# Decode attention: loading K and V two heads per transfer, their rows interleaved

## The chip, the cores and the metric

One core of one Trainium2 chip. The metric is device microseconds of one execution, each version run several times. A kernel's "ratio" below is the mean time of its runs over the mean of the other kernel's runs of the same rounds, so it is not quite the ratio of the medians that are quoted beside it.

## The reference, cut to what matters

Two layers, each an attention block and a small MLP, run on one token. Every attention block reads the last 4,096 rows of the K and of the V cache of all 32 heads, 192 bf16 each:

```python
W = min(4096, max(256, Sk // 4))                 # 4096
k = k_cache[:, :, Sk - W:, :]; v = v_cache[:, :, Sk - W:, :]
scores = einsum("bhqd,bhkd->bhqk", q, k) * Dh ** -0.5
o = einsum("bhqk,bhkd->bhqd", softmax(scores), v)
# ... then  @ wo, and the MLP: layernorm, w3, gelu, w4.  Both layers share K, V and all weights.
```

One head's K or V is 4,096 × 192 × 2 B = 1.5 MB. The kernel reads 216 MB in all, and there is one query: nearly everything is a load.

## The kernel before

The arena is 11 "cells" of 12,288 B per partition. One head's K or V fills a cell: partition p holds 32 consecutive cache rows, so a transfer is 128 packets of 12,288 contiguous bytes, 8 for each of the 16 DMA engines.

```python
def load_k(layer, h):
    t = take(("k", layer, h))                    # the cell that was freed first
    nc.sync.dma_start(t[:], A_k_cache[0, h, s0:Sk, :].rearrange("(p j) d -> p (j d)", p=P))
    return t
```

VectorE transposes K in 32×32 blocks of 4-byte words (two bf16 together), so that a score matmul reads every second bf16 of a row, in four quarters of a head:

```python
nc.vector.transpose(Tu, Ku[:, :, q * NY:(q + 1) * NY])
# ... scores():
nc.tensor.matmul(ST_ps[r:r + QW, :]..., lhsT=Q[:, n, :], rhs=T4[:, :, f, :, t], ...)
```

The product with V has two columns of probabilities at a time, and one transpose of the result for each head:

```python
nc.tensor.matmul(O_ps[r:r + 2, :], lhsT=PT[:, hq, 2 * i:2 * i + 2],
                 rhs=v_pair(V, h, 2 * i * Dh, 2 * Dh), start=(i < 4), stop=(i >= NB - 4))
# ... after the 16 matmuls of a head:
nc.vector.transpose(o_sb[:], O_ps.rearrange("p (e a c) -> p e c a", e=2, c=NA))
```

Layer 0 keeps the transposed K of heads 0 to 6 and parts of V in on-chip memory for layer 1, so cells are scarce around the layer change. The loads are one stream in a fixed order, all issued by SP; each waits only for its cell to be free. At the end of layer 1 come wo, w3 and w4.

Of the kernel before, what the change touches and what calls it, by code (L numbers as in the profile page):

```python
# [8 lines left out]
BF16 = mybir.dt.bfloat16  # L9
# [26 lines left out]
def kernel(  # L36
# [38 lines left out]
    NKX = 6  # L75
    NKEEP, NCELL = 7, 11
# [13 lines left out]
    cells = ctx.enter_context(tc.tile_pool(name="cells", bufs=1))  # L90
# [15 lines left out]
    kx = const.tile([P, VN], BF16, name="kx")  # L106

# [3 lines left out]
    free = deque(range(NCELL))  # L111
    cell_of = {}

    def take(key):
        i = free.popleft()
        cell_of[key] = i
        return cells.tile([P, FREE], BF16, tag=f"cell{i}", name=f"cell{i}")

    def give(key):
        free.append(cell_of.pop(key))  # L120
# [7 lines left out]
    def load_k(layer, h):  # L128
        t = take(("k", layer, h))
        nc.sync.dma_start(t[:], A_k_cache[0, h, s0:Sk, :].rearrange("(p j) d -> p (j d)", p=P))  # L130
        return t

    def load_v(layer, h):
        t = take(("v", layer, h))
        src = A_v_cache[0, h, s0:Sk, :].rearrange("(p j) d -> p (j d)", p=P)
        cut = (2 * VW,) if h == VP else (FREE - VN,) if h == VX else ()
        if layer == 1 and h in GROUPS[layer][-1][-2:]:
            cut = FREE // 2,
        i = 0
        for e in cut + (FREE,):  # L140
            kept_v = h == VP or h == VX and i > 0
            if layer == 0 or not kept_v:
                nc.sync.dma_start(v_pair(t, h, i, e - i), src[:, i:e])
            i = e
        return t
# [23 lines left out]
    def load_w3(layer):  # L169

        t = take(("w3", layer))
# [9 lines left out]
    def load_w4(layer):  # L181

        t = take(("w4", layer))
# [19 lines left out]
    def layer_stream(layer):  # L203
# [3 lines left out]
        def k_item(hh):  # L207
            if layer == 0 or hh >= NKEEP:
                seq.append(("k", layer, hh))

        def v_item(hh):
            if (layer, hh) == (1, VC):
                return
# [48 lines left out]
    ones = const.tile([P, P], F32, name="ones")  # L262
    nc.vector.memset(ones[:], 1.0)
    Lf = wx_sb[:, 0:2 * P].bitcast(F32).rearrange("p (j i) -> p j i", j=4)
    nc.gpsimd.memset(Lf, 0.0)
    for base in (0, -1, -64, -65):
# [10 lines left out]
    even = const.tile([P, 1], F32, name="even")  # L277
    nc.vector.reduce_sum(even[:], ident[:].rearrange("p (m two) -> p m two", two=2)[:, :, 0], axis=AX.X)
    lo = const.tile([P, 1], F32, name="lo")
    nc.vector.reduce_sum(lo[:], ident[:, 0:64], axis=AX.X)  # L280
    maskq = const.tile([P, 4], F32, name="maskq")
    nc.vector.tensor_tensor(out=maskq[:, 0:1], in0=lo[:], in1=even[:], op=ALU.mult)
    nc.vector.tensor_tensor(out=maskq[:, 1:2], in0=lo[:], in1=maskq[:, 0:1], op=ALU.subtract)
    nc.vector.tensor_tensor(out=maskq[:, 2:3], in0=even[:], in1=maskq[:, 0:1], op=ALU.subtract)
    nc.vector.tensor_scalar(out=maskq[:, 3:4], in0=lo[:], scalar1=-1.0, scalar2=1.0, op0=ALU.mult, op1=ALU.add)
    nc.vector.tensor_tensor(out=maskq[:, 3:4], in0=maskq[:, 3:4], in1=maskq[:, 2:3], op=ALU.subtract)
    blkm = const.tile([P, NM], F32, name="blkm")
    nc.vector.reduce_sum(blkm[:], ident[:].rearrange("p (m b) -> p m b", m=NM), axis=AX.X)
# [3 lines left out]
    eps1 = const.tile([P, 1], F32, name="eps1")  # L292
    nc.vector.memset(eps1[:], eps)

    hm = const.tile([P, QH], F32, name="hm")
    nc.vector.tensor_reduce(out=hm[:], in_=ident[:].rearrange("p (q x m) -> p x q m", q=4, m=NM)[:, 0:QH],
                            op=ALU.add, axis=AX.XY)

    QW = QH * NM
    QHEAD = NCOL * QW  # L300
    QSLOT = QH * (QHEAD + NM)
# [10 lines left out]
    xT = const.tile([P, ND], F32, name="xT0")  # L312
    xT_ps = psm.tile([P, ND], F32, tag="psm")
    nc.tensor.transpose(xT_ps[:, :], x_rf, ident[0:ND, 0:ND])
    rs0 = const.tile([P, 1], F32, name="rs0")
    nc.vector.tensor_scalar(out=xT[:], in0=xT_ps[:], scalar1=1.0, scalar2=None, op0=ALU.mult,
# [3 lines left out]
    def ln_center(x, rowsum):  # L320

        mean_ps = psm.tile([P, 1], F32, tag="psm")
        nc.tensor.matmul(mean_ps[:], lhsT=ones[:], rhs=rowsum[:, 0:1], start=True, stop=True)
# [3 lines left out]
        xcf = big.tile([P, ND], F32, name="xcf")  # L327
        nc.vector.scalar_tensor_tensor(out=xcf[:], in0=mean_ps[:, 0:1].broadcast_to([P, ND]), scalar=-1.0 / D,
                                       in1=x[:], op0=ALU.mult, op1=ALU.add)
        junk = sm.tile([P, ND], F32, tag="ln_junk")  # L330
        ssq = sm.tile([P, 1], F32, tag="ln_ssq")
        nc.scalar.activation(junk[:], xcf[:], ACTF.Square, accum_out=ssq[:, 0:1])

        def total():
            var_ps = psm.tile([P, 1], F32, tag="psm")
            nc.tensor.matmul(var_ps[:], lhsT=ones[:], rhs=ssq[:, 0:1], start=True, stop=True)
            return var_ps
# [3 lines left out]
    def power(var, mul, bias, tag):  # L341

        ln_t = big.tile([P, 1], F32, tag=tag + "_ln")
        nc.scalar.activation(ln_t[:], var, ACTF.Ln, bias=bias, scale=mul)
        r = big.tile([P, 1], F32, tag=tag)
        nc.scalar.activation(r[:], ln_t[:], ACTF.Exp, scale=-0.5)
# [7 lines left out]

    kept = {}
    area = [None, 0]

    def transpose_quart(layer, h, q):
# [5 lines left out]
        Ku = Kn[:].bitcast(U32).rearrange("p (j y b) -> p j y b", j=NJ4, b=32)  # L364
# [4 lines left out]
        else:  # L369
            if area[0] is None:  # L370
                area[0] = take(("area", layer))
            T = area[0][:, area[1] * QUART:(area[1] + 1) * QUART]
            area[1] = (area[1] + 1) % NT
# [6 lines left out]
    def qproj_steps(c, xc, part=None, row=None):  # L380
# [49 lines left out]
        def block():  # L430
            nh = n * P // Dh
            h0 = 4 * (t0 - c * QT) // NCOL
            diag = Qblk[:, c % 2].rearrange("p (h r) -> p h r", h=QH)[:, h0:h0 + nh, 0:QHEAD]
# [6 lines left out]

    def scores(h, Ts, q0, ST_ps, hq):

        ng = NGK // NT
        Q = Qblk[:, h // QH % 2, hq * QHEAD:(hq + 1) * QHEAD].rearrange("p (f x) -> p f x", x=QW)
# [26 lines left out]
    def softmax_steps(n, ST_ps, sc):  # L471
        held = {}

        def part_max():
            pm = big.tile([P, 1], F32, name="pm")
            nc.vector.tensor_reduce(out=pm[:], in_=ST_ps, op=ALU.max, axis=AX.X)
            held["pm"] = pm

        def turn_max():
            pmT_ps = psm.tile([1, P], F32, tag="psm")  # L480
            nc.tensor.transpose(pmT_ps[0:1, :], held["pm"][:, 0:1], ident[:, :])
            held["pmT"] = pmT_ps

        def full_max():
            ngm = big.tile([1, 2 * QH], F32, name="ngm")
            nc.vector.tensor_reduce(out=ngm[:], in_=held["pmT"][0:1, :].rearrange("o (q x m) -> o x q m", q=4, m=NM),
                                    op=ALU.max, axis=AX.XY, negate=True)
            held["PrT"] = o_bytes[:, SW:2 * SW]

            wide = held["PrT"][0:1, :].bitcast(F32)  # L490
            nc.vector.tensor_scalar(  # L491
                out=wide.rearrange("o (q x m) -> o q x m", q=4, m=NM),
                in0=ngm[:].unsqueeze(1).unsqueeze(3).broadcast_to([1, 4, 2 * QH, NM]),
                scalar1=sc[0:1, 0:1], scalar2=None, op0=ALU.mult)
            held["w"] = wide

        def spread_max():
            nb_ps = psm.tile([P, 1], F32, tag="psm")
            nc.tensor.matmul(nb_ps[:], lhsT=held["w"],  # L499
                             rhs=ones[0:1, 0:1], start=True, stop=True)  # L500
            nb_sb = big.tile([P, 1], F32, name="nb_sb")
            nc.scalar.copy(nb_sb[:], nb_ps[:])  # L502
            Pr = o_bytes[:, 0:SW]
            lpart = big.tile([P, 1], F32, name="lpart")
            nc.scalar.activation(out=Pr, in_=ST_ps, func=ACTF.Exp,  # L505
                                 bias=nb_sb[:, 0:1], scale=sc[:, 0:1], accum_out=lpart[:, 0:1])
            held["Pr"], held["l"] = Pr, lpart

        def turn_p():
            nc.vector.transpose(held["PrT"], held["Pr"])  # L510
            lh = big.tile([P, QH], F32, name="lh")
            nc.vector.tensor_scalar(out=lh[:], in0=hm[:], scalar1=held["l"][:, 0:1], scalar2=None, op0=ALU.mult)
            held["lh"] = lh

        def swap():
            ng = NGK // NT
            PT_ps = psm.tile([P, n, NJ4, NGK], F32, tag="psm")
            src = held["PrT"].rearrange("p (g j i) -> p i j g", g=ng, j=NJ4)
# [4 lines left out]
            PT = big.tile([P, n, NJ4 * NGK], BF16, name="PT")  # L523
            nc.scalar.copy(PT[:].rearrange("p h c -> p (h c)"), PT_ps[:].rearrange("p h j g -> p (h j g)"))  # L524
            l_ps = psm.tile([P, QH], F32, tag="psm")
            nc.tensor.matmul(l_ps[:], lhsT=ones[:], rhs=held["lh"][:], start=True, stop=True)  # L526
            held["lps"] = l_ps
            return PT

        def recip():  # L530
            lq = big.tile([P, QH], F32, name="lq")
            rl = sm.tile([P, 1], F32, name="rl")
            nc.vector.scalar_tensor_tensor(out=lq[:], in0=held["lps"][:], scalar=1.0, in1=blkm[:],
# [24 lines left out]
    def pv(layer, h, hq, PT, mid=None):  # L558
# [3 lines left out]
        NB = NJ4 * NGK // 2  # L562
        for i in range(NB):
            if mid is not None and i == NB // 2:
                mid()
            r = 32 * (i % 4)
            nc.tensor.matmul(O_ps[r:r + 2, :], lhsT=PT[:, hq, 2 * i:2 * i + 2],  # L567
                             rhs=v_pair(V, h, 2 * i * Dh, 2 * Dh), start=(i < 4), stop=(i >= NB - 4))
# [3 lines left out]
        else:  # L572
            give(("v", layer, h))
        nc.vector.transpose(o_sb[:], O_ps.rearrange("p (e a c) -> p e c a", e=2, c=NA))  # L574

    def o_fold(h, oT, rl, add=False):
        r = slice(32 * (h % QH), 32 * (h % QH) + 32)
        oT_ps = psm.tile([P, NA], F32, tag="psm")
        if not add:
            for e in range(2):  # L580
                nc.tensor.matmul(oT_ps[r, :], lhsT=Lq[:], rhs=o_sb[:, e, :, e], start=(e == 0), stop=(e == 1))  # L581
# [3 lines left out]
        nc.vector.tensor_add(o2[:], o_sb[:, 0, :, 0], o_sb[:, 1, :, 1])  # L585
# [53 lines left out]
    def attention(layer, x_cur, rs_cur, x_new, z_new, rs_new, ss_new):  # L639
# [3 lines left out]
        junk = sm.tile([P, ND], F32, tag="ln_junk")  # L643
# [3 lines left out]
        sc = sm.tile([P, 1], F32, name="sc")  # L647

        def softmax_scale():
            rstd = power(total()[:, 0:1], 1.0 / D, eps1[:], "rstd")  # L650
            nc.vector.tensor_scalar(out=sc[:], in0=rstd[:], scalar1=scale, scalar2=None, op0=ALU.mult)
# [6 lines left out]
        def S(h, half, ST_ps, hq):  # L658
# [5 lines left out]
            scores(h, [Th.pop((h, q)) for q in (2 * half, 2 * half + 1)], 2 * half, ST_ps, hq)  # L664
# [321 lines left out]
```

## Time and profile before

| | before |
|---|---|
| time, median of the first 3 runs | 524.71 us (524.38 to 525.29) |
| span of the profiled execution | 522.9 us |
| load queue's packets, share of 16 engines' span | 23,908, 99.0% |
| PE, DVE, ACT busy | 63%, 56%, 9% |

The page of the kernel before: the span, the engines' busy time, then in 40 slices the busy share of the DMA engines in tenths and what they moved, then the packets: the load queue and the queue that fetches instructions (packets, MB, share of 16 engines).

```profile
span 522.9 us, 9589 instructions
PE 330.3 (63%) x4146; PEld 195.5 (37%) x4146; DVE 294.6 (56%) x589; ACT 49.5 (9%) x175; POOL 4.0 (1%) x16
...
DMA  8999999999999999999999999999999999999996
GB/s 345 429 424 425 423 426 427 423 424 423 427 421 428 424 422 428 423 423 423 423 399 398 388 425 427 424 424 423 426 423 424 426 423 426 421 427 425 420 410 237
...
q1 hardware_dynamic: 23908, 216.48, 99.0%
q8 instruction: 32, 0.52, 0.4%
```

The transfers are the bound: every slice but the first and the last is full, at about 424 GB/s. The three slices near 390 are full as well; w3, w4 and short pieces have packets of 1,280 to 3,072 B there.

Five stretches of the kernel before in the table of stretches (start:end and length in us, busy time and number of instructions of PE, PEld, DVE, ACT and POOL, the granted TensorE clock, DMA share, GB/s):

```profile
100.00:125.00 25.00, 16.88 (x183) 9.46 (x185) 17.74 (x33) 2.79 (x9) 0.00 (x0) 0.64 1.01 424
125.00:150.00 25.00, 15.94 (x169) 8.99 (x166) 15.98 (x30) 2.80 (x9) 0.00 (x0) 0.70 1.01 423
150.00:175.00 25.00, 14.46 (x166) 8.26 (x155) 14.25 (x24) 1.03 (x4) 0.00 (x0) 0.70 1.01 427
...
275.00:300.00 25.00, 18.26 (x357) 12.23 (x356) 8.01 (x38) 3.48 (x16) 0.00 (x0) 0.50 1.01 393
...
425.00:450.00 25.00, 17.89 (x197) 9.82 (x189) 15.56 (x28) 3.06 (x10) 0.00 (x0) 0.59 1.01 425
```

The DMA share stands at 1.01, and so it does over 13 to 120 us and 120 to 250 us. In one short stretch that could be an accident of counting, since a packet counts whole where it starts; over 100 us and more, a share above 1 says that packet records overlap in time.

Costly groups of the kernel before (line, engine, operation, output and inputs, shape, count, then busy us and mean ns, then idle time before them and its cause):

```profile
L451 PE MATMUL ST_ps<-cell_277,Qblk 128*16 128x256 bf16 x600 | 70.1, 392 | 50.9 <-DVE cell_277 L375 34.3 <-DVE pm L476 13.8 <-DVE o_1599 L585 0.5
...
L574 DVE STREAM_TRANSPOSE o_sb<-O_ps 128x384 f32<-128x384 f32 x64 | 37.2, 582 | 112.4 <-PE O_ps L567 112.3
```

The end of the chain of waits (start us, us, what), then the output's transfer from the timeline:

```profile
481.22 24.05 DMA cell_5324<-in_A_v_cache_dram
505.28 10.63 DMA cell_5423<-in_B_w_dram
```

```profile
520.81 0.30 SPq L955 DMA_DIRECT2D out_dram<-Lb  x1
```

The end hangs on the last V (landed at 505.28 us) and then on w3 (at 515.91 us); the MLP and the output follow.

### The profile page before, as it was taken

What the parts mean: (1) busy time and instruction counts of PE and PEld (TensorE: products, weight loads), DVE (VectorE), ACT (ScalarE), POOL (GpSimd) and SP (SyncE); (2) the same over time, 40 slices, a digit from 0 to 9 for tenths busy, and PEclk for the clock granted to TensorE, in tenths of its full rate; (3) what the DMA queues carried; (4) which work ended last, traced back from release to release, by engine and by line L of the source; (5) the groups of instructions that cost most, each with busy time, mean ns of one, the idle gap of its engine ahead of it and who ended that gap; (6) DMA issues with size and microseconds to landing.
All of it is one profiled execution on the core that took longest, in us unless ns stands there. A gap on an engine that the chain in (4) does not pass through costs nothing.

```text
span 522.9 us, 9589 instructions
## 1 busy us (share of the span) xinstructions
PE 330.3 (63%) x4146; PEld 195.5 (37%) x4146; DVE 294.6 (56%) x589; ACT 49.5 (9%) x175; POOL 4.0 (1%) x16
## 2 busy tenths in 40 slices
PE   2057668666665566767655866667675666647675
PEld 2023334333332333434333544334343333425344
DVE  2067656666574664556624264766576866654722
ACT  1000101010010100001011101001010101001011
POOL 2000000000000000000000000000000000000000
PEclk9995656567677776576555567657787865766755
DMA  8999999999999999999999999999999999999996
GB/s 345 429 424 425 423 426 427 423 424 423 427 421 428 424 422 428 423 423 423 423 399 398 388 425 427 424 424 423 426 423 424 426 423 426 421 427 425 420 410 237
DMA packets 23949, 217.08 MB, mean 415 GB/s; under 512 B 2532, under 2 KB 3044, under 8 KB 8420
## 3 DMA queue, kind: packets, MB, share of 16 engines
q1 hardware_dynamic: 23908, 216.48, 99.0%
q8 instruction: 32, 0.52, 0.4%
q14 instruction: 9, 0.07, 0.0%
HBM read 216.47 MB, written 0.00 MB: 414 GB/s over the span
## 4 chain that ended last, share of the span: by engine, by line
DMA 43%; PE 27%; DVE 25%; issue 2%; ACT 2%; SPq 1%; DVEq 0%; ACTq 0%
PE ST_ps L451 11%; DVE cell_3304 L375 9%; PE O_ps L567 8%; DVE cell_277 L375 8%; DMA cell_1925<-in_A_k_cache_dram 6%; DMA cell_4933<-in_A_k_cache_dram 5%; DMA cell_1629<-in_A_k_cache_dram 5%; DMA cell_1329<-in_A_k_cache_dram 5%; DMA cell_4637<-in_A_k_cache_dram 5%; DMA cell_5324<-in_A_v_cache_dram 5%; DMA cell_275<-in_A_k_cache_dram 4%; DVE o_sb L574 2%; DMA cell_2478<-in_A_v_cache_dram 2%; DMA cell_2690<-in_A_v_cache_dram 2%; DMA cell_5423<-in_B_w_dram 2%
## 5 line engine op out<-in xcount | busy, mean ns | idle before, releaser
L451 PEld LDWEIGHTS <-Qblk 128*16 128x16 bf16 x1536 | 86.1, 113 | 178.6 <-issue 151.1
L451 PE MATMUL ST_ps<-cell_277,Qblk 128*16 128x256 bf16 x600 | 70.1, 392 | 50.9 <-DVE cell_277 L375 34.3
L574 DVE STREAM_TRANSPOSE o_sb<-O_ps 128x384 f32<-128x384 f32 x64 | 37.2, 582 | 112.4 <-PE O_ps L567 112.3
L451 PE MATMUL ST_ps<-cell_3304,Qblk 128*16 128x256 bf16 x600 | 67.3, 382 | 43.5 <-DVE cell_3304 L375 28.3
L567 PEld LDWEIGHTS <-PT 128*2 128x2 bf16 x1024 | 47.2, 102 | 21.8 <-issue 11.3
L510 DVE STREAM_TRANSPOSE o_sb<-o_sb 128x256 bf16<-128x256 bf16 x16 | 7.1, 445 | 34.1 <-ACT o_sb L505 25.0
L582 ACT ACTIVATE oT<-oT_ps,rl 32x6 bf16<-32x6 f32 x40 | 10.3, 258 | 163.5 <-PE oT_ps L581 157.1
L581 PEld LDWEIGHTS oT_ps<-o_sb,Lq 128*32 128x32 f32 x160 | 13.2, 145 | 19.9 <-issue 16.1
L581 PE MATMUL oT_ps<-o_sb,Lq 128*32 128x6 f32 x160 | 13.9, 196 | 10.4 <-DVE o_sb L574 9.9
L587 ACT ACTIVATE oT<-oT_ps,rl 32x6 bf16<-32x6 f32 x24 | 6.2, 258 | 108.4 <-PE ST_ps L451 93.7
L405 PE MATMUL qT_ps<-xc,wq_sb 128*128 128x1 bf16 x210 | 7.2, 165 | 13.4 <-DMA wq_sb<-in_A_wq_dram 12.5
L419 DVE TENSOR_TENSOR Xq<-qT_ps,maskq 128x24 bf16<-128x24 f32 (+1 forms) x18 | 2.8, 157 | 18.3 <-PE qT_ps L405 18.3
L521 PE MATMUL PT_ps<-o_sb,Eq 128*32 128x32 bf16 x256 | 7.2, 237 | 9.2 <-DVE o_sb L510 4.0
L394 PE MATMUL qr_ps<-wq_sb,xc 128*1 128x384 bf16 x90 | 12.8, 433 | 0.0
L521 PEld LDWEIGHTS <-Eq 128*32 128x32 bf16 x256 | 5.5, 111 | 18.9 <-issue 18.8
L405 PEld LDWEIGHTS <-wq_sb 128*128 128x128 bf16 x210 | 6.8, 104 | 14.8 <-DMA wq_sb<-in_A_wq_dram 13.6
L502 ACT COPY nb_sb<-nb_ps 128x1 f32<-128x1 f32 x16 | 2.5, 159 | 97.6 <-PE nb_ps L499 97.6
L526 PE MATMUL l_ps<-lh,ones 128*128 128x4 f32 x32 | 8.5, 336 | 4.9 <-ACT PT L524 4.9
L499 PEld LDWEIGHTS nb_ps<-ones,o_sb 1*128 1x128 f32 x32 | 7.6, 292 | 7.4 <-issue 5.5
L526 PEld LDWEIGHTS l_ps<-lh,ones 128*128 128x128 f32 x32 | 7.1, 275 | 7.5 <-ACT PT L524 7.1
L499 PE MATMUL nb_ps<-ones,o_sb 1*128 1x1 f32 x32 | 8.9, 345 | 1.5 <-DVE o_sb L491 1.5
L426 PE MATMUL Qrep_ps<-Xq,Lb 128*128 128x24 bf16 (+1 forms) x18 | 3.2, 179 | 10.4 <-DVE Xq L419 10.1
(376 smaller groups left out, 533.2 us busy)
## 6 DMA issues: line engine op xcount, KB each, us to landing
wq_sb<-in_A_wq_dram SPq DMA_DIRECT2D x5, 1536.0 KB, 12.7
cell_275<-in_A_k_cache_dram SPq DMA_DIRECT2D x1, 1536.0 KB
cell_309<-in_A_k_cache_dram SPq DMA_DIRECT2D x1, 1536.0 KB, 26.4
cell_346<-in_A_k_cache_dram SPq DMA_DIRECT2D x1, 1536.0 KB, 27.1
cell_376<-in_A_k_cache_dram SPq DMA_DIRECT2D x1, 1536.0 KB
cell_444<-in_A_k_cache_dram SPq DMA_DIRECT2D x1, 1536.0 KB, 30.8
cell_503<-in_A_v_cache_dram SPq DMA_DIRECT2D x1, 1536.0 KB, 30.8
cell_505<-in_A_k_cache_dram SPq DMA_DIRECT2D x1, 1536.0 KB, 30.8
```

The source lines that it names most:

```text
L375: nc.vector.transpose(Tu, Ku[:, :, q * NY:(q + 1) * NY])
L394: nc.tensor.matmul(qr_ps[32 * i:32 * i + 1, :], lhsT=xc[:, kc:kc + 1], rhs=wq_sb[:, kc, t0 * P + i * N:t0 * P + (i + 1) * N], start=(kc == ...
L405: nc.tensor.matmul(qT_ps[:, tl:tl + 1], lhsT=wq_sb[:, kc, t * P:(t + 1) * P], rhs=xc[:, kc:kc + 1], start=(kc == 0), stop=(kc == ND - 1))
L451: nc.tensor.matmul(ST_ps[r:r + QW, :].rearrange("p (g i) -> p g i", g=ng), lhsT=Q[:, n, :], rhs=T4[:, :, f, :, t], start=(hq == 0 and n == ...
L499: nc.tensor.matmul(nb_ps[:], lhsT=held["w"], rhs=ones[0:1, 0:1], start=True, stop=True)
L510: nc.vector.transpose(held["PrT"], held["Pr"])
L521: nc.tensor.matmul(PT_ps[32 * m:32 * (m + 1), :, :, ng * q:ng * (q + 1)], lhsT=Eq[:, q, :], rhs=src[:, m:QW:NM], start=True, stop=True)
L526: nc.tensor.matmul(l_ps[:], lhsT=ones[:], rhs=held["lh"][:], start=True, stop=True)
L567: nc.tensor.matmul(O_ps[r:r + 2, :], lhsT=PT[:, hq, 2 * i:2 * i + 2], rhs=v_pair(V, h, 2 * i * Dh, 2 * Dh), start=(i < 4), stop=(i >= NB - 4))
L574: nc.vector.transpose(o_sb[:], O_ps.rearrange("p (e a c) -> p e c a", e=2, c=NA))
L581: nc.tensor.matmul(oT_ps[r, :], lhsT=Lq[:], rhs=o_sb[:, e, :, e], start=(e == 0), stop=(e == 1))
L582: nc.scalar.activation(oT[r, :], oT_ps[r, :], ACTF.Copy, scale=rl[r, 0:1])
```

## The change

Its intent: fewer, longer packets. Heads 8 to 31 in layer 0 and 12 to 31 in layer 1 are loaded in pairs. Even partitions hold 64 rows of the first head, odd partitions 64 rows of the second, 24,576 B each, so that a pair is 128 packets in place of 256. A pair needs two adjacent cells, so cells are now slices of one tile, handed out by a written plan. The transposes stay as they were; the score matmul reads one head's columns at every 8 bytes in place of 4. Probabilities for a pair have four columns (zeros for the other head's rows), two heads share an output transpose, and the end of layer 1 is reordered. Small tiles are packed into one, which makes room to keep a little more of V (NKX 6 to 8).

```diff
-    NKX = 6
-    NKEEP, NCELL = 7, 11
+    NKX = 8
+    NKEEP, NCELL, NSINGLE = 7, 11, (8, 12)
+    arena = const.tile([P, NCELL * FREE], BF16, name="arena")
+    plan = deque([ 0, 2, 3, 5, 7, 9, 0, 3, ... ])          # cut
+    def load_pair(kind, cache, layer, h):
+        t = take((kind, layer, h), 2)
+        src = cache[0, h:h + 2, s0:Sk, :].rearrange("h (r j) d -> r h (j d)", r=P // 2)
+        cuts = (FREE, 3 * FREE // 2) if (kind, layer, h) == ("v", 1, H - 2) else ()
+        i = 0
+        for e in cuts + (2 * FREE,):
+            nc.sync.dma_start(t[:, i:e], src[:, :, i:e])
+            i = e
+    # scores_pair(): ... for e in range(2): rhs=T2[:, f, e, t]   (every fourth bf16)
-            nc.tensor.matmul(O_ps[r:r + 2, :], lhsT=PT[:, hq, 2 * i:2 * i + 2],
+            nc.tensor.matmul(O_ps[r:r + M, :], lhsT=PT[:, hq, i, :],          # M = 4 for a pair
+        if paired and h % 2 == 0:
+            return                                           # one transpose for two heads
# cut: packing of small tiles, the softmax steps for pairs, the reordered end of layer 1
```

## The prediction

> **What bounds the kernel.** The transfers. The slice table shows the 16 DMA engines at 99% and 420–429 GB/s in nearly every slice; the queue table gives the load queue 99.0% of 16 engines' span (517 of 522.9 us). PE is busy 63%, DVE 56%. The rest is the start (the first 13 us move 343 GB/s, by the table of stretches) and about 5 us of tail after the last weights land. In the issue table K and V land 23–31 us after issue in most of both layers, 8–15 us near the layer change, so 2 to 8 cells of 1.5 MB (3.7 us each) are in flight; compute doesn't set the pace, though half of the chain of waits is compute. The stretch 262–300 us isn't idle either: DMA share 0.99 to 1.02 at 391–399 GB/s, as its packets are smaller.
>
> **What a packet costs.** The trace's records, median per packet on one engine: 2,560 B 105 ns, 7,680 B 294, 9,984 B 376, 12,288 B 462. The slope is 0.0365–0.037 ns/B (about 27.3 GB/s), the intercept 11–14 ns. 12,288/462 × 16 is 425 GB/s, the rate seen, so the intercept is paid in throughput. The Trainium skill ("DMA: Bandwidth & Descriptors", Where 436 GB/s comes from) puts the ports' ceiling at 435 GB/s; the trace agrees so far, with at most 429 in a slice.
>
> **What the change does.** 43 pairs of K or V loads become one transfer each of 128 packets of 24,576 B, in place of 256 of 12,288 B; the last V pair drops 128 more packets. Estimate from the fit: a 24,576 B packet takes 910–913 ns in place of 924.
> - Packets: 5,504 × 11–14 ns / 16 = 3.8–4.8 us saved, 0.1 more from the last pair.
> - 44 fewer transfers, so fewer completion writes (9 ns each per engine): at most 0.4 us.
> - NKX 6 to 8 keeps 98 KB more of V: 0.2 us.
>
> While pairs stream: about 430 GB/s in place of 425. Nearly all of it is on the critical path, as the DMA engines never idle. Start, layer change (single heads) and tail transfers stay.
>
> **Costs beside it.** PE has the same number of score and PV matmuls; score columns are read every 8 bytes in place of 4 (now 382–392 ns a matmul; I expect under 10% change). DVE loses 22 output transposes of 582 ns; K transposes stay at about 950 ns; ACT gains one copy of ~0.27 us in each paired group. A pair needs two adjacent cells, so loads run ahead less: I estimate from the order of takes and gives 17–25 us of transfer time in place of 28–32, still ample. None of this should reach the time.
>
> **Prediction.** 520.0 us, 8 in 10 between 518.6 and 523.5; −0.9%. Chances: faster by over 2% 0.02, within 2% 0.92, slower by over 2% 0.06.
>
> **Right if the profile shows:** about 5,600 fewer packets; 24,576 B packets near 911 ns; slices of pairs at 429–432 GB/s, the middle still 390–400; DMA still 99%; DVE busy down about 10 us without gain from it; tail within 0.5 us of before.
>
> **Wrong if:** the source's outer dimension of 64 rows spreads packets unevenly over engines or ports (pair packets well over 920 ns: slower by many per cent); the engines are at their limit already, so that 24 KB take 2 × 462 ns (524 us); pairs wait for two adjacent cells, so that DMA slices fall below 99% in pair stretches; or the last V pair, landing later, pushes attention past w3's landing and lengthens the tail by 1–2 us.

## The result, and the profile after

The changed kernel took 522.26 us in the median (521.27 to 522.80, 4 runs) against 524.96 us (4 runs): ratio 0.9947, 95% interval 0.9933 to 0.9961. Two later sets of five rounds gave 0.9955 each. So it is faster by 2.4 to 2.8 us, inside the predicted range, but the gain is little over half of the forecast 4.7 us.

The page of the changed kernel:

```profile
span 519.5 us, 9509 instructions
PE 314.4 (61%) x4146; PEld 173.9 (33%) x4146; DVE 284.3 (55%) x582; ACT 53.4 (10%) x186; POOL 4.0 (1%) x16
...
DMA  8999999999999999999999999999999999999995
GB/s 345 437 429 437 416 436 427 425 435 414 438 432 423 433 416 429 427 408 424 424 421 390 391 425 427 428 432 425 430 429 425 431 427 431 423 432 430 425 404 225
...
q1 hardware_dynamic: 17572, 216.38, 98.7%
```

There are 6,336 fewer packets on the load queue: 5,632 of data and 704 completion writes (packets of 4 B that report a landing, 16 for each transfer). The same five stretches:

```profile
100.00:125.00 25.00, 16.14 (x204) 8.38 (x201) 15.03 (x30) 3.41 (x11) 0.00 (x0) 0.80 1.01 431
125.00:150.00 25.00, 13.64 (x144) 6.29 (x144) 15.15 (x28) 2.78 (x9) 0.00 (x0) 0.73 1.00 426
150.00:175.00 25.00, 13.16 (x174) 6.53 (x173) 14.29 (x26) 1.65 (x6) 0.00 (x0) 0.79 1.01 430
...
275.00:300.00 25.00, 17.71 (x416) 13.56 (x414) 9.18 (x42) 3.48 (x16) 0.00 (x0) 0.62 0.99 389
...
425.00:450.00 25.00, 14.96 (x198) 7.88 (x196) 13.19 (x25) 3.41 (x11) 0.00 (x0) 0.77 1.01 433
```

Where pairs stream, the rate is higher: the six stretches from 25 to 175 us average 428.5 GB/s (426 to 431) in place of 424.7 (423 to 427). One stretch alone, such as the 433, says less: one round of 16 packets of 24,576 B more or less is 16 GB/s in 25 us, and 30 GB/s in a slice of 13 us, which is why slices swing more, from 408 to 438. Around the layer change nothing is gained. The groups:

```profile
L503 PE MATMUL ST_ps<-arena,Qblk 128*16 128x256 bf16 x1056 | 120.3, 405 | 87.2 <-DVE cols L542 43.8 <-DVE arena L428 42.0 <-DVE o_3783 L698 0.2
...
L678 DVE STREAM_TRANSPOSE o_sb<-O_ps 128x384 f32<-128x384 f32 x42 | 24.4, 581 | 96.0 <-PE O_ps L668 96.0
```

The pairs' score matmul with its wider stride records 405 ns against 392 (382 in the other large group of the kernel before), although the granted clock was higher (0.80 against 0.64 in the stretch at 100 us). The output transposes fell from 64 to 42, and DVE's busy time by 10.3 us. The end of the chain and the output's transfer:

```profile
480.90 20.52 DMA arena<-in_A_v_cache_dram
501.44 10.70 DMA arena<-in_B_w_dram
```

```profile
517.18 0.32 SPq L1083 DMA_DIRECT2D out_dram<-Lb  x1
```

The end is the same sequence, 3.8 us earlier at the last V and at w3, and 3.6 us at the output. This profiled execution happened to be the fastest of its four.

### The profile page after: what moved, and what is told of

It is laid out like the page before. It is cut to its first block, busy times and chain, and to the rows that moved or that the text cites. A ratio compares the mean times of both kernels' runs of the same rounds, so it can differ in the third digit from the quotient of the medians. Undisturbed runs are those within 1.5% of the kernel's fastest.

```text
span 519.5 us, 9509 instructions
## 1 busy us (share of the span) xinstructions
PE 314.4 (61%) x4146; PEld 173.9 (33%) x4146; DVE 284.3 (55%) x582; ACT 53.4 (10%) x186; POOL 4.0 (1%) x16
## 4 chain that ended last, share of the span: by engine, by line
DMA 51%; PE 24%; DVE 20%; issue 2%; ACT 2%; SPq 1%; DVEq 0%; ACTq 0%
DMA arena<-in_A_v_cache_dram 28%; DMA arena<-in_A_k_cache_dram 21%; DVE arena L428 14%; PE ST_ps L503 8%; PE O_ps L668 6%; PE ST_ps L517 3%; DMA arena<-in_B_w_dram 2%; DVE o_sb L678 1%; PE nb_ps L576 1%; DVE o_sb L585 1%; PE y_ps L748 1%; PE l_ps L627 1%; PE qT_ps L458 1%; PE y_ps L1059 1%; ACT o_sb L580 1%
## 5 line engine op out<-in xcount | busy, mean ns | idle before, releaser
L428 DVE STREAM_TRANSPOSE arena<-arena 128x768 uint32<-128x768 uint32 x228 | 204.1, 946 | 41.0 <-DMA arena<-in_A_k_cache_dram 38.8
L503 PE MATMUL ST_ps<-arena,Qblk 128*16 128x256 bf16 x1056 | 120.3, 405 | 87.2 <-DVE cols L542 43.8
L503 PEld LDWEIGHTS <-Qblk 128*16 128x16 bf16 x1056 | 50.5, 105 | 146.9 <-issue 110.2
L668 PE MATMUL O_ps<-arena,PT 128*4 128x384 bf16 (+1 forms) x952 | 90.3, 441 | 12.3 <-DMA arena<-in_A_v_cache_dram 11.9
L678 DVE STREAM_TRANSPOSE o_sb<-O_ps 128x384 f32<-128x384 f32 x42 | 24.4, 581 | 96.0 <-PE O_ps L668 96.0
L517 PE MATMUL ST_ps<-arena,Qblk 128*16 128x256 bf16 x480 | 41.7, 357 | 21.3 <-DVE arena L428 14.2
L668 PEld LDWEIGHTS <-PT 128*4 128x4 bf16 (+1 forms) x960 | 37.4, 99 | 31.7 <-issue 18.4
L517 PEld LDWEIGHTS <-Qblk 128*16 128x16 bf16 x480 | 22.7, 106 | 37.9 <-issue 30.6
L695 ACT ACTIVATE oT<-oT_ps,rl 32x6 bf16<-32x6 f32 x40 | 10.3, 258 | 145.2 <-PE oT_ps L694 103.7
L694 PEld LDWEIGHTS oT_ps<-o_sb,Lq 128*32 128x32 f32 x160 | 8.5, 134 | 16.4 <-issue 14.2
L627 PE MATMUL l_ps<-cols 128*128 128x4 f32 x32 | 8.0, 320 | 8.2 <-ACT PT L620 6.9
L627 PEld LDWEIGHTS l_ps<-cols 128*128 128x128 f32 x32 | 6.6, 257 | 10.6 <-ACT PT L620 8.5
L620 ACT ACTIVATE PT<-PT_ps,cols 128x128 bf16<-128x128 f32 x20 | 6.3, 364 | 36.2 <-PE PT_ps L612 36.2
```

What stands on the lines that cost most here:

```text
L503: nc.tensor.matmul(ST_ps[r:r + QW, :].rearrange("p (g i) -> p g i", i=P // 2), lhsT=Qblk[:, h // QH % 2, x:x + QW], rhs=T2[:, f, e, t], st ...
L517: nc.tensor.matmul(ST_ps[r:r + QW, :].rearrange("p (g i) -> p g i", g=ng), lhsT=Q[:, n, :], rhs=T4[:, :, f, :, t], start=(hq == 0 and n == ...
L620: nc.scalar.activation(PT[:, :, :, c], PT_ps[:].rearrange("p x (i e) -> p x i e", e=2), ACTF.Copy, scale=side)
L627: nc.tensor.matmul(l_ps[:], lhsT=ones, rhs=held["lh"][:], start=True, stop=True)
L668: nc.tensor.matmul(O_ps[r:r + M, :], lhsT=PT[:, hq, i, :], rhs=v_pair(V, h, 2 * i * Dh, 2 * Dh), start=(i < 4 and not (paired and h % 2)), ...
L694: nc.tensor.matmul(oT_ps[r, :], lhsT=Lq[:], rhs=o_sb[:, e, :, x + e], start=(e == 0), stop=(e == 1))
```

## The experiments

The question is why only 2.4 to 2.8 us came of a forecast 4.7. Theory A: a packet costs less beyond its bytes than forecast. Theory B: it costs what was forecast, and pairs waiting for two cells or new work give back some 2 us. Theory C: the gain comes from the other parts of the change.

Several figures below are worked out from the trace's packet records. The records carry no engine number, so each packet's start was matched with the nearest end on one of 16 engines, which may lie a few ns after the start. This gives the time from one packet's start to the next on an engine. "Lag" is the time by which an engine's last load ends before the last of all, averaged over the 16; it needs only the 16 ends.

### The changed kernel again, and its packets undone in two ways, and no pairs at all

These four ran on the same chip and share the runs of the kernel before (524.94 us, 11 runs).

> The changed kernel again, for a tighter figure beside its variants. Theory A (what a packet costs beyond its bytes is smaller than forecast: the records overlap by 3 ns, so 8 to 9 ns a packet are really paid, and nothing is given back elsewhere): 522.2 us, 0.5% under the kernel before. Theory B (a packet does cost 11 to 14 ns, 4.3 us are saved on packets, and some 2 us are given back, by pairs waiting for two adjacent cells and at the layer change): the same 522.2 us, so this run alone does not tell them apart.

Measured: 522.81 us (6 runs), ratio 0.9955 (0.9940 to 0.9970).

Each pair in two transfers of half rows:

```diff
-        cuts = (FREE, 3 * FREE // 2) if (kind, layer, h) == ("v", 1, H - 2) else ()
+        cuts = (FREE, 3 * FREE // 2) if (kind, layer, h) == ("v", 1, H - 2) else (FREE,)
```

> Every pair loaded in two transfers of half rows: packets of 12,288 B again, 5,504 more of them, everything else as in the changed kernel. Theory A: 43 x 128 x 8.5 ns / 16 = 2.9 us more than the changed kernel, 525.1 us, about the kernel before. Theory B: 43 x 128 x 12.5 ns / 16 = 4.3 us more plus what is given back stays, 526.5 to 527 us, clearly slower than the kernel before. Theory C (the gain comes from the packing, the rearranged end or the larger kept part, not from packets): within 0.5 us of the changed kernel.

Measured: 526.29 us (6 runs), ratio 1.0022 (1.0009 to 1.0034), 3.5 us over r_after. Alone this would have spoken for something between A and B. But its profile has a lag of 2.45 us (the kernel before: 1.45), and it was already 0.67 us behind when the first 10 MB had landed, with slower packets just where the pairs begin. Why they are slower there was not settled. Between these two places, from 10 to 214 MB, it took 484.8 us, as did e_rows12 below; the changed kernel took 481.9 (mean of six profiles). That is theory A's 2.9 us. But this variant changed more than the packet size at both ends, and the next one is the cleaner test.

One transfer for each pair, two heads side by side in a partition (wrong sums, since the computing still takes the rows as interleaved; the result stayed within the comparison's tolerance, but that comparison would not have caught such an error):

```diff
-        for e in cuts + (2 * FREE,):
+        if not cuts:
+            plain = cache[0, h:h + 2, s0:Sk, :].rearrange("h (p j) d -> p h (j d)", p=P)
+            nc.sync.dma_start(t.rearrange("p (h x) -> p h x", h=2), plain)
+            cuts, i = (), 2 * FREE
+        for e in cuts + ((2 * FREE,) if i == 0 else ()):
```

> One transfer for each pair as in the changed kernel, but the heads not interleaved, so rows of 12,288 B; the sum is wrong on purpose, the work the same. Theory A with packets alone counting: as e_halves, 525 us. If it is the number of transfers (issue and completion) that counts, it stays at 522.2 us. Theory B: 526 to 527 us.

Measured: 525.14 us (5 runs), ratio 1.0005 (0.9992 to 1.0018). Packet size alone, with the number of transfers, the order and all the computing as in the changed kernel, is worth (1.0005 − 0.9955) × 524.9 = 2.6 us, the whole gain. Halving the number of transfers is worth nothing that can be seen: this kernel has as few as the changed one and is no faster than the kernel before, or than e_singles below (1.0008), which keeps the packing without pairs. Theory B's 526 to 527 us did not come.

No pairs; the packing and the larger kept part stay, the old order of cells and the old end come back (the edit is cut here):

```diff
-    NKEEP, NCELL, NSINGLE = 7, 11, (8, 12)
+    NKEEP, NCELL, NSINGLE = 7, 11, (H, H)
-        i = plan.popleft()
+        i = free.popleft()                 # first freed, first taken, as before
+        if layer == 1 and h in GROUPS[layer][-1][-2:]:
+            cut = FREE // 2,
-            fast = hurry and layer == 1
+            fast = False                   # the old end of layer 1
```

> The changed kernel with no pairs at all: cells handed out in order as before, the old end, the packed tiles and the larger kept part stay. Theory A: 0.2 us under the kernel before, 524.6 us. Theory B: the same 524.6. Theory C: 522 to 523 us.

Measured: 525.22 us (6 runs), ratio 1.0008 (0.9993 to 1.0024). Theory C falls: without pairs there is no gain. The reordered end is undone here too, but e_rows12 keeps it and gains nothing either.

### A dose, and the cost by itself

In this call the kernel before took 525.13 us (7 runs).

```diff
+        if not cuts:
+            plain = cache[0, h, s0 - W:Sk, :].rearrange("(u p j) d -> p u (j d)", u=4, p=P)
+            nc.sync.dma_start(t.rearrange("p (u x) -> p u x", u=4), plain)
```

> A dose: the pairs again in one transfer each, but of rows of 6,144 B (taken from one head's older rows, so a wrong sum on purpose), 16,512 packets more than the changed kernel, 11,008 more than e_rows12. Theory A with the 6 to 7 ns a packet that e_rows12 less the changed kernel gives (2.3 us x 16 / 5,504): 7 us over the changed kernel, about 529.5 us. Theory B with 12.5 ns a packet: 12.9 us over it, 535.5 us. If only the step from 12 to 24 KB counts, it stays at e_rows12's 525 us.

Measured: 531.79 us (4 runs), ratio 1.0129 (1.0109 to 1.0149). Against the changed kernel's ratio of 0.9955 that is 1.74% or 9.1 us for 16,512 packets over 16 engines: 8.9 ns a packet. Neither figure of the expectation was right: A's 7 us is too small, B's 12.9 us is further off. Theory A's own figure had moved by then, from 8 to 9 ns a packet before r_after to 6 to 7 here and 6 in the next expectation; what was measured is where it began.

The second kernel has no computing, only loads in twelve stretches:

```python
ORDER = [1, "pair", 1 / 2, 2, 1 / 4, 1, "pair", 2, 1 / 2, 4, 1 / 4, 1]
# n >= 1: n rows a partition in each 1.5 MB transfer; 1/2, 1/4: one row over 2 or 4 cells
```

> The disputed cost by itself: loads alone, no computing, in twelve stretches of 37.7 MB, rows of 12,288 B, pairs interleaved (24,576 B), one head's rows of 24,576 B, 6,144 B, 49,152 B, 12,288, pairs, 6,144, 24,576, 3,072, 49,152 and 12,288 B; zeros as the result on purpose. Theory A (6 ns a packet beyond 0.0369 ns a byte, from packet starts in the kernels' traces): 411 GB/s for 3,072 B, 421 for 6,144, 427 for 12,288, 430 for 24,576 and 432 for 49,152. Theory B (12.5 ns): 395, 416, 427, 433 and 436. If interleaving two heads costs something of itself, the pairs fall below the one head's rows of the same size; if computing slows the transfers, 12,288 B rows run clearly over the 425 GB/s of the kernels.

Stretches of this kernel in the table of stretches (busy time of DVE and POOL, clock, DMA share, GB/s), in order: 12,288 B, pairs, one head's 24,576 B, 6,144 B, 3,072 B, 49,152 B:

```profile
10.00:80.00 70.00, 0.00 (x0) 0.00 (x0) 1.00 1.01 427
98.00:170.00 72.00, 0.00 (x0) 0.00 (x0) 1.00 1.01 431
186.00:256.00 70.00, 0.00 (x0) 0.00 (x0) 1.00 1.00 430
273.00:346.00 73.00, 0.00 (x0) 0.00 (x0) 1.00 1.02 418
...
805.00:882.00 77.00, 0.00 (x0) 0.00 (x0) 1.00 1.03 402
899.00:970.00 71.00, 0.00 (x0) 0.00 (x0) 1.00 1.00 433
```

The rates lie between the two theories. The median times from start to start on an engine say why:

| row | start to start | record's duration | twice this, less the next line |
|---|---|---|---|
| 3,072 B | 122 ns | 126 ns | 9 ns |
| 6,144 B | 235 ns | 239 ns | 9 ns |
| 12,288 B | 461 ns | 465 ns | 9 ns |
| 24,576 B | 913 ns | 916 ns | 10 ns |
| 49,152 B | 1,816 ns | 1,820 ns | |

One straight line fits: 0.0368 ns a byte ((1,816 − 122) / 46,080), which is 435 GB/s over 16 engines, and 9 ns for each packet. The records last 3 to 4 ns longer than the start-to-start time: they overlap. This is what the DMA share shows, 1.03 for the smallest rows (4 of 122 ns) and 1.00 for the largest. Interleaving costs nothing of itself (431 against 430 GB/s), and 12,288 B rows run at 427 GB/s without any computing against 424 to 425 in the kernels, where fetching instructions takes another 0.4% of the engines' time (queue q8 of the page before). That leaves little that computing could cost the transfers.

What a row costs an engine with completion writes and occasional slower packets counted in was taken from the mean start of 128 packets near the beginning of a stretch and of 128 near its end. It is 460.4, 461.2 and 461.2 ns in the three stretches of 12,288 B and 913.0 in all four of 24,576 B: 7.8 to 9.4 ns saved for each two rows, 8.9 in the mean. 43 pairs are then worth 43 × 128 × 8.9 / 16 = 3.1 us. (A first count, of the bytes landed between two instants, had given 10.8 ns and the 3.7 us of the next expectation; such a count moves with a round of packets.) The kernels agree: from 30 to 220 and 330 to 480 us the mean time from start to start is 463.5 ns for 12,288 B (2 profiles of the kernel before) and 917.9 for 24,576 B (6 of the changed kernel), 9.1 ns for each two rows.

### Where the rest goes

3.1 us from the rows and 0.2 us from the larger kept part would be 3.3; 2.4 to 2.8 were timed. Runs of the changed kernel also spread more (521.3 to 523.6 us).

> More profiles of the unchanged changed kernel, whose runs spread over 2.3 us (521.3 to 523.6 us) where most of the kernel before lie within 0.4. What the packets save by e_stream (3.7 us) is more than the 2.4 to 2.8 us timed; the two profiles so far are of faster runs. If the rest is lost in how far apart the 16 engines end (D), the slower profiles have a mean lag of engines behind the last one above the 1.6 to 1.8 us seen, by as much as they are longer. If it is lost at the layer change (E), the lag is the same and the DMA idle time between 280 and 300 us is larger.

> As r_after2: the time of load from first to last packet, the idle time at the layer change and the spread of the engines' ends, for one more execution.

> As r_after2: once more the load period, the idle time at the layer change and the spread of the engines' ends, for a further execution of the changed kernel.

> A second profile of the kernel before, for the same figures: a mean lag near 1.45 us, idle time at the layer change as in the first profile, span near 523 us.

With the two earlier profiles and that of r_after5 (below) there are six of the changed kernel and two of the kernel before. "214 MB landed" is counted from the first load.

| execution | span us | 214 MB landed | first load to last | lag | idle at the layer change |
|---|---|---|---|---|---|
| before | 522.88 | 509.67 | 517.32 | 1.45 | 1.16 |
| r_before2 | 522.61 | 509.42 | 517.02 | 1.40 | 1.26 |
| after | 519.50 | 506.23 | 513.74 | 1.63 | 1.36 |
| r_after2 | 519.51 | 506.32 | 513.64 | 1.40 | 1.18 |
| r_after3 | 519.93 | 506.51 | 514.07 | 1.63 | 1.41 |
| r_after | 520.15 | 506.57 | 514.33 | 1.81 | 1.42 |
| r_after5 | 520.60 | 506.70 | 514.78 | 2.20 | 1.20 |
| r_after4 | 520.71 | 506.29 | 514.85 | 2.67 | 1.22 |

("Idle at the layer change": gaps of over 20 ns between an engine's packets, 225 to 300 us, mean of 16.) The three longest executions are those with the largest lag, in the same order. The idle time at the layer change does not order them. D holds for the spread between executions and E does not. r_after2, 3 and 4 ran on one chip, so it is not a difference between chips.

The clearest pair is r_after2 and r_after4: by 214 MB the two are level, and yet the second ends 1.2 us later. The end of the chain of waits of r_after2, then of r_after4:

```profile
481.35 20.25 DMA arena<-in_A_v_cache_dram
501.62 10.67 DMA arena<-in_B_w_dram
```

```profile
482.18 20.66 DMA arena<-in_A_v_cache_dram
502.85 10.65 DMA arena<-in_B_w_dram
```

A transfer has landed only when the slowest of its 16 engines is done. In r_after4 two engines end 1.0 us and more after the other 14 (in r_after2 six end within 0.3 us), so the last V and w3 land 1.2 us later although as many bytes have come. The Trainium skill ("DMA: Bandwidth & Descriptors", iDMA fabric) says in passing, within an explanation that it calls unconfirmed, that "a bulk load runs at the pace of its slowest engine"; these two traces agree.

The account in means of these profiles (2 before, 6 after):

| | us |
|---|---|
| saved when 214 MB have landed (509.54 to 506.44) | 3.1 |
| saved from first load to last (517.17 to 514.24; lag 1.43 to 1.89) | 2.9 |
| saved in the span (522.75 to 520.07) | 2.7 |

The 3.1 us that e_stream gives for the rows are there by 214 MB (at equal bytes the larger kept part does not enter), if not evenly: from 90 to 140 MB, the single heads and the layer change, the changed kernel loses 0.2 us (1.6 ahead at 90 MB, 1.4 at 140). The larger lag takes about 0.5 us at the end, which the 0.2 us for the larger kept part only half offsets. Between the output's issue and the end of the span lie 2.07 us before and 2.32 us after (522.88 − 520.81, 519.50 − 517.18); this 0.25 us was seen but not explained. Why the lag is larger and varies more with long rows was not settled: e_rows12, with rows of 12,288 B and everything else of the change, had 1.52 us in its one profile, but e_halves had 2.45 with the same row length.

### A version that might have beaten both

If a packet costs 9 ns, the short rows of the MLP's weights are the next to merge. Here w4's rows go from 2,560 and 1,280 B to 5,120 and 3,840 B (one piece of 1,280 B stays):

```diff
-        pairs = B_w4.rearrange("(k p two) n -> p k (two n)", p=P, two=2)
+        fours = B_w4.rearrange("(k p four) n -> p k (four n)", p=P, four=4)
-                    f0 = 2 * P * (fc // 2) + fc % 2
+                    f0 = 4 * P * (fc // 4) + fc % 4
```

> A version that may beat both: the changed kernel with the second MLP weight in rows of four (5,120 and 3,840 B in place of 2,560 and 1,280 B; hidden units numbered to match, the first weight's columns read at every 8 bytes), 640 packets fewer. By the 9 ns a packet of e_stream (theory A): 0.36 us under the changed kernel of the same call, 0.5 us under at most, which the scatter of the engines' ends (1.2 us between executions) may hide. If strided weight loads cost, the mixer's first products grow over 1.4 us in layer 1 and it is slower by as much.

> The changed kernel beside e_fours on the same chip: ratio to the kernel before near 0.995, so about 522.4 us; its profile's mean lag of engines between 1.4 and 2.7 us, and the span longer or shorter with it.

Measured against the same runs of the kernel before (525.04 us, 9 runs): e_fours 523.22 us, ratio 0.9966 (0.9953 to 0.9978); r_after5 522.44 us, ratio 0.9955 (0.9941 to 0.9968). It has 656 packets fewer (16,916 on the load queue), and is not faster; the intervals overlap, so it is not shown to be slower either. Its one profile has a lag of 2.61 us. The chain of waits explains one part: in layer 1 the end hangs on w3's landing, and w4 arrives in its shadow, so only the 384 packets of layer 0 could count, 0.2 us, which these runs can't resolve. The feared cost of strided weight loads did not come: from the first MLP product to the output's row took 6.8 us in both profiles. But its one profile, 0.3 us behind r_after5's at 115 MB and 0.1 us ahead at 125, where layer 0's w4 lands, is 1.1 us behind at 160 MB: after the layer change its loads are issued later (two of K at 302.82 and 308.83 us against 299.52 and 304.82). So the loss may lie there and not in the rows; one profile of each can't show it, and why was not looked for. The changed kernel stays the best.

## Why the prediction was right or wrong

- **"The transfers" bound the kernel, and what counts is the packets: right.** Undoing the packet size alone (e_rows12) takes the whole gain away, and four times the packets (e_rows6) cost 9.1 us.
- **"the intercept 11–14 ns": this is the step that failed.** It was fitted to the durations of the records. Records overlap by 3 to 4 ns, so a packet occupies its engine for less than its record. Loads alone show 9 ns. So the rows gave 3.1 us where the prediction's terms for packets, the last pair and completions add up to 4.3 to 5.3; that is over half of the 2 us that were missing. The check in the prediction, "12,288/462 × 16 is 425 GB/s, the rate seen", seemed to confirm the durations. In the trace of the kernel before, the median start-to-start time is 459 ns, but completion writes (6 ns after every 8 packets) and occasional slower packets (mean start to start 465 ns, idle gaps included) bring the rate back to 425 by chance. A DMA share above 1, of which the prediction quotes 1.02 for one stretch, was the sign of the overlap and was not read as one.
- **"44 fewer transfers … at most 0.4 us" was added on top.** A completion write takes 6 ns from start to start, not 9, so 0.26 us, and the 3.1 us have it counted in.
- **"Nearly all of it is on the critical path": nearly.** By 214 MB all 3.1 us are kept. The account overlooked that the end waits for the slowest engine, not for the mean of 16; the lag rose from 1.43 to 1.89 us, which takes 0.5 us back. Why it rose stays open.
- **Costs beside it: right.** DVE's busy time fell by 10.3 us with no gain from it, the score matmuls' records grew 3 to 6%, and waiting for adjacent cells shows nowhere: gaps of over 20 ns between an engine's packets add up to 0.7 us from 30 to 220 us and 0.6 us from 330 to 480 us, in the kernel before and in the changed one alike. This is the plainest evidence against theory B.
- **The signs it named:** 5,632 fewer packets of data (about 5,600 forecast), 24,576 B packets with a median record of 915 ns (911), pair stretches of 428.5 GB/s in the mean (slices of 429 to 432 forecast), the middle at 389 (390 to 400), the time from the last load to the end within 0.3 us of before. Each is close, and still the sum was off by 2 us: small differences of large numbers. 915 in place of 911 ns is a third of the forecast gain.
- **The feared causes did not come:** no uneven spread from the 64-row outer dimension (pairs and one head's rows run at 431 and 430 GB/s), no limit before 431 GB/s.

## What to carry to other kernels

When transfers are the bound and every engine is full, each packet costs about 9 ns beside its bytes, here from 3 to 48 KB; going from 12 to 24 KB rows gave 1.0% of the rate and going on to 48 KB would give half a percent more, while merging transfers without longer rows gave nothing. Take a packet's cost from start to start, never from its record's length, and look at the DMA share: over 1.00 in a long stretch, it says that the records overlap. A small saving spread over 16 engines reaches the end only through the slowest of them, so compare several profiles before explaining half a microsecond.

## What the Trainium skill lacked or had wrong

- "DMA: Bandwidth & Descriptors", Where 436 GB/s comes from: the note there says that for transfers between HBM and on-chip memory the HBM side, about 358 GB/s, binds. One core alone read 431 GB/s from HBM with 24,576 B rows and 433 with 49,152 B rows. The note lacks the condition that the page's Measured section has: about 358 holds with both cores of an HBM domain streaming. The page's ceiling of 435 GB/s agrees with the slope found (435).
- The same page, Why small descriptors are slow, treats a packet's fixed cost as a matter of a few hundred bytes. The cost was there at every size from 3,072 to 49,152 B: 9 ns a packet, 402 GB/s at 3,072 B, 418 at 6,144, 427 at 12,288.
- The same page, Rules for kernel authors, asks for 1 MiB or more in each transfer; it does not say whether still larger ones gain. From 1.5 to 3 MB, with the queue always full and the rows as long as before, nothing changed (ratio 1.0005 for e_rows12, 1.0008 for e_singles).
- No page says how far the 16 engines drift apart at the end of an even load: the mean lag was 1.4 to 2.7 us between six executions of one program, and the three with the largest were the longest.
- No page says that the profile's packet records of one engine overlap, by 3 to 4 ns here, so that durations overstate the cost of a packet.
